# A branch of its own for each step of an expert's first layer, weight copies placed one by one, and rank operations in later experts

## The chip, the cores and the metric

The kernel runs on one core of a Trainium2 chip. The metric is the device time of one launch in microseconds (us). A core has a matrix engine (TensorE, PE in the rows, with its weight loads as PEld), three engines for elementwise work (VectorE = DVE, ScalarE = ACT, GpSimd = POOL), a queue engine (SyncE = SP), and DMA queues that move data between main memory and the on-chip buffer (SBUF). TensorE writes its products into eight banks of an accumulator memory (PSUM). Each engine works off its own list of instructions in order and waits on semaphores for the others.

## The reference

Clustered attention, then a mixture of experts over its result, then a gated layer over that. Only the middle part bears on the change:

```python
expert_idx = np.argmax(logits, axis=1)          # logits = x @ w_gate, x is 1536 x 512
...
for i in range(N):                              # first come, first served
    e = expert_idx[i]
    if counts[e] < capacity:                    # capacity 384
        disp[e, counts[e]] = x[i]; pos[i] = counts[e]; counts[e] += 1; keep[i] = True
h = np.maximum(np.einsum('ecd,edf->ecf', disp, w1), 0.0)   # w1: 8 x 512 x 1024
y = np.einsum('ecf,efd->ecd', h, w2)                       # w2: 8 x 1024 x 512
out[i] = gate_w[i] * y[expert_idx[i], pos[i]]              # for kept tokens
```

So there are eight experts of two layers each, 512 to 1024 with a Relu and 1024 to 512, and each token goes through one of them. All data are float32.

## The kernel before

The attention takes the first 270 us or so, the experts run from 284 to 476 us, and the gated layer (`g`, `v` and `o` in the rows) follows.

**Products.** To keep float32's precision each operand is held as a high part and a low part (names ending in h and l, or an index 0 and 1 in `X` and `H`), and a product is the sum of high by high, high by low and low by high. An expert with up to 208 tokens streams high and low side by side, 2 x 208 columns (or 2 x 176, if it has up to 176 tokens), so that one pass of the high weights gives two partial results, and a pass of the low weights over the high part adds to the first (`both`, lines 877 and 878). What is left of such a *merged* step is to add the two halves: ScalarE copies the second half out of PSUM (`half`, line 902) and VectorE adds it to the first (line 903). An expert with more tokens takes the *wide* form with 384 columns and three passes (`prod`, line 869). The number of tokens is only known at run time, so every engine branches on it (`arms`, lines 855 and 858). In this data experts 0, 3, 5 and 6 take the form for 208, experts 1, 2 and 4 that for 176, and expert 7 the wide one.

**An expert.** The first layer has four steps of two 128-column blocks each (`hp`). `l1` runs two steps in one branch: products and half additions of both, and only then, for both, the Relu into the high part of `H` on ScalarE (line 915) and the low part of `H` on VectorE (line 919). Between the two calls stand the transposes of the next expert's token rows (`xt`, tile `xp`, line 840, ScalarE and VectorE copies into `X` at lines 845 and 846) and the weight copies. The second layer has two steps (`yp`), each in a branch of its own (`l2`): products, half addition, and the high and low part of the result `Y` (lines 932 and 936). A second-layer product takes the eight 128-row blocks of `H` in order, and so each `yp` reads first what the first step of the first layer made, and last what its last step made.

**Weights.** An expert has eight chunks of 128 x 1024 weights: 0 to 3 make `W1`, 4 to 7 make `W2` (4 and 5 for the first `yp`, 6 and 7 for the second). `split` takes one: a ScalarE copy rounds it to the high part (line 813), a subtraction gives the low part (line 814) on VectorE for `W1` and on GpSimd for `W2`, and SyncE then loads a later chunk into the raw buffer that came free (line 804). The gathered token rows of the next expert (`xr`, 768 KB) are requested on ScalarE's queue at the start of each expert (line 825).

**Order.** There is no planner: each engine takes its instructions as the code is written. `run` writes for each expert: `l1` of steps 0 and 1, `split` 4 and 5, `l1` of steps 2 and 3, (in expert 5 the products of `tokens`), in expert 0 the rank operations, `xt` of the next expert, `split` 6 and 7, `l2` step 0, `split` 0 and 1 of the next expert, `l2` step 1, `split` 2 and 3 of the next expert. The rank operations are 8 short VectorE instructions (`ranks`, lines 712 to 718, on 128 x 96 and 128 x 12 elements) that number the tokens, and 7 more (`invert`, lines 731 to 743) that prepare the inverse list; nothing needs them before `hots` and `tokens` in expert 5.

**PSUM.** `hp`, `xp` and `yp` share one ring of four buffers, so that a step waits until the buffer of four allocations earlier has been read out.

## Time and profile before

| | |
|---|---|
| median of 3 runs | 783.03 us (782.71 to 783.65) |
| profiled execution | 781.34 us, of which 779.6 us from the first to the last instruction |
| mean granted TensorE clock | 0.996 |
| TensorE busy | 747.8 us, 96% of the span |
| VectorE, ScalarE, GpSimd busy | 513.4, 397.9, 268.7 us (66%, 51%, 34%) |
| experts, 284.0 to 476.4 us | 192.4 us, TensorE busy 180.5 |

The profiled execution is one launch. Its rows give start and length of instructions; in brackets stands how long the engine sat idle before one and what ended that. A busy TensorE row may overlap the next, so lengths of stretches on it are best taken from start to start. The profiled execution's own time is 1.7 us under the median of the runs, and 1.7 us of it lie outside the span.

### The profile page before, as it was taken

What the parts mean: (1) busy time and instruction counts of PE and PEld (TensorE: products, weight loads), DVE (VectorE), ACT (ScalarE), POOL (GpSimd) and SP (SyncE); (2) the same over time, 40 slices, a digit from 0 to 9 for tenths busy, and PEclk for the clock granted to TensorE, in tenths of its full rate; (3) what the DMA queues carried; (4) which work ended last, traced back from release to release, by engine and by line L of the source; (5) the groups of instructions that cost most, each with busy time, mean ns of one, the idle gap of its engine ahead of it and who ended that gap; (6) DMA issues with size and microseconds to landing.
All of it is one profiled execution on the core that took longest, in us unless ns stands there. A gap on an engine that the chain in (4) does not pass through costs nothing.

```text
span 779.6 us, 12354 instructions
## 1 busy us (share of the span) xinstructions
PE 747.8 (96%) x4311; PEld 622.9 (80%) x4311; DVE 513.4 (66%) x881; ACT 397.9 (51%) x744; POOL 268.7 (34%) x244
## 2 busy tenths in 40 slices
PE   7999999999999987999999999999999999999996
PEld 6777777777777677999999998788888888888885
DVE  5677878788787747556655555777676766767433
ACT  5776777786776535567666633354222222222110
POOL 6121220210220275443492452444323333233244
PEclk9999999999999999999999999999999999999999
DMA  8847857626532263687777543323112222110012
GB/s 204 209 104 210 205 178 212 158 60 165 121 124 67 82 219 121 207 258 245 235 246 230 191 137 109 104 86 106 57 55 71 66 67 69 55 54 1 1 54 108
DMA packets 93337, 102.34 MB, mean 131 GB/s; under 512 B 30304, under 2 KB 77408, under 8 KB 93248
## 3 DMA queue, kind: packets, MB, share of 16 engines
q1 hardware_dynamic: 88384, 89.33, 39.9%
q0 software_dynamic: 1920, 6.29, 2.1%
q10 hardware_dynamic: 2944, 5.54, 2.0%
q8 instruction: 55, 0.90, 0.5%
q14 instruction: 34, 0.28, 0.1%
HBM read 68.21 MB, written 12.58 MB: 104 GB/s over the span
## 4 chain that ended last, share of the span: by engine, by line
PE 47%; POOL 5%; DVE 4%; issue 3%; DMA 2%; ACT 2%; POOLq 0%; ACTq 0%; SPq 0%; DVEq 0%
PE o L1102 12%; PE v L1082 11%; PE g L1082 11%; PE hp L877 4%; POOL W2l L814 4%; PE hp L869 2%; PE yp L869 2%; PE yp L877 2%; PE hp L878 2%; DMA raw<-in_moe_w 1%; PE yp L878 1%; DVE cb L1060 1%; POOL out L1113 1%; DMA xr<-moe_rows 0%; DMA moe_rows<-x,rslot 0%
## 5 line engine op out<-in xcount | busy, mean ns | idle before, releaser
L814 POOL TENSOR_TENSOR W2l<-raw,W2h 128x1024 fp32r<-128x1024 f32 x32 | 76.5, 2415 | 86.5 <-ACT W2h L813 86.4
L342 DVE TENSOR_REDUCE nm<-s 128x1 f32<-128x768 f32 x96 | 91.1, 949 | 11.6 <-PE s L339 10.6
L352 ACT ACTIVATE P<-s,nm 128x768 f32<-128x768 f32 x96 | 86.6, 902 | 13.3 <-DVE nm L342 10.3
L368 PE MATMUL t<-ident,P 128*128 128x128 f32 x576 | 81.1, 274 | 0.8 <-ACT PT L371 0.6
L1091 POOL TENSOR_TENSOR ghl<-u,ghh 128x512 fp32r<-128x512 f32 x36 | 50.0, 1389 | 75.3 <-ACT ghh L1090 75.3
L368 PEld LDWEIGHTS t<-ident,P 128*128 128x128 f32 x576 | 68.5, 140 | 7.8 <-DVE PT L373 2.3
L877 PE MATMUL yp<-H,W2h 128*128 128x416 f32 (+1 forms) x224 | 67.7, 369 | 6.7 <-DVE X L846 3.5
L387 PE MATMUL acc<-PT,ldv 128*64 128x384 f32 x384 | 69.7, 495 | 0.0
L877 PE MATMUL hp<-X,W1h 128*128 128x416 f32 (+1 forms) x224 | 65.2, 362 | 2.0 <-issue 1.3
L339 PE MATMUL s<-Ak,Aq 128*128 128x384 f32 x192 | 58.5, 386 | 3.4 <-ACT P L352 3.1
L1110 DVE TENSOR_TENSOR acc<-o,acc 128x512 f32<-128x512 f32 x60 | 41.2, 692 | 31.0 <-PE o L1102 31.0
L371 ACT COPY PT<-t 128x384 f32<-128x384 f32 x96 | 45.8, 477 | 29.6 <-PE t L368 29.4
L1088 DVE TENSOR_TENSOR u<-sg,g 128x512 f32<-128x512 f32 x36 | 24.7, 687 | 54.1 <-ACT sg L1087 54.1
L878 PE MATMUL yp<-H,W2l 128*128 128x208 f32 (+1 forms) x224 | 57.6, 257 | 2.1 <-POOL W2l L814 1.8
L1090 ACT CAST ghh<-u 128x512 fp32r<-128x512 f32 x36 | 22.4, 622 | 67.6 <-DVE u L1089 67.6
L878 PE MATMUL hp<-X,W1l 128*128 128x208 f32 (+1 forms) x224 | 56.0, 250 | 0.0
L373 DVE COPY PT<-t 128x384 f32<-128x384 f32 x96 | 52.3, 545 | 0.9 <-PE t L368 0.9
L339 PEld LDWEIGHTS s<-Ak,Aq 128*128 128x128 f32 x192 | 29.0, 189 | 28.3 <-ACT P L352 20.2
L339 PE MATMUL s<-kB,qB 80*128 80x384 f32 (+1 forms) x192 | 50.3, 342 | 1.0 <-ACT kB L274 0.7
L877 PEld LDWEIGHTS yp<-H,W2h 128*128 128x128 f32 x224 | 42.8, 191 | 8.6 <-ACT H L915 4.3
L1060 DVE SCALAR_TENSOR_TENSOR cb<-raw,cb 128x512 uint32<-128x512 uint32 x36 | 47.4, 1318 | 1.2
L387 PEld LDWEIGHTS acc<-PT,ldv 128*64 128x64 f32 x384 | 24.9, 136 | 28.8 <-issue 27.9
(251 smaller groups left out, 1866.4 us busy)
## 6 DMA issues: line engine op xcount, KB each, us to landing
raw<-in_moe_w SPq DMA_DIRECT2D x64, 512.0 KB, 4.4
Ak<-Hk SPq DMA_DIRECT2D x32, 192.0 KB, 4.1
moe_rows<-zero SPq DMA_DIRECT2D x8, 768.0 KB, 5.4
raw<-in_moe_w_gate SPq DMA_DIRECT2D x12, 512.0 KB, 3.5
raw<-in_moe_w_val SPq DMA_DIRECT2D x12, 512.0 KB, 3.5
raw<-in_moe_w_out SPq DMA_DIRECT2D x12, 512.0 KB, 3.7
xr<-moe_rows ACTq DMA_DIRECT2D x7, 768.0 KB, 6.7
ldq<-in_q SPq DMA_DIRECT2D x16, 192.0 KB, 3.9
```

The lines of the kernel that those rows point to most:

```text
L339: nc.tensor.matmul(ps[:, c, 0:HS], lhsT=ql[:, qs], rhs=kr[:, c * HS:(c + 1) * HS], start=a == 0, stop=a == 1)
L342: nc.vector.tensor_reduce(out=nm, in_=ps[:, :, 0:HS], axis=AX.XY, op=ALU.max, negate=True)
L352: nc.scalar.activation(out=P, in_=ps[:, :, 0:HS], func=AF.Exp, bias=nm, accum_out=self.pairs[n]["sum"][:, i, r:r + 1])
L368: nc.tensor.transpose(ps[:, jj, :], P[:, a, jj * 128:(jj + 1) * 128], self.ident)
L373: nc.vector.tensor_copy(PT[:, js, cs], ps)
L387: nc.tensor.matmul(acc[c * D:(c + 1) * D], lhsT=v[:, c * HJ + j], rhs=PT[:, c * HJ + j, :], start=j == 0, stop=j == HJ - 1, tile_position= ...
L814: (nc.vector if i < 4 else nc.gpsimd).tensor_tensor(out=l, in0=t, in1=h.bitcast(F32), op=ALU.subtract)
L877: self.nc.tensor.matmul(out[:, :, 0:w], lhsT=W[0][:, k, cols], rhs=mov[:, :, k, 0:w], start=k == 0, stop=False)
L878: self.nc.tensor.matmul(out[:, 0, 0:w], lhsT=W[1][:, k, cols], rhs=mov[:, 0, k, 0:w], start=False, stop=k == ks - 1)
L1060: v.scalar_tensor_tensor(out=b, in0=Hw, scalar=0xC0000000, in1=b, op0=ALU.bitwise_and, op1=ALU.bitwise_or)
L1082: nc.tensor.matmul(p, lhsT=W[a], rhs=self.Y[b][:, k, ts], start=i == 0, stop=i == 3 * self.KD - 1)
L1102: nc.tensor.matmul(p[t], lhsT=h[a][:, fc, t * 128:(t + 1) * 128], rhs=W[b][:, fc], start=fc == 0 and i == 0, stop=fc == 1 and i == 2)
```

## The change

`l1` now takes one step. Its branch first does the Relu and low part of the step in front (`hidden(mp - 1)`), then the products and half addition of its own step. The last step's Relu and low part get a branch of their own. `split` 4 stands behind step 0, `split` 5 behind step 1, `split` 6 behind step 3, in front of the last `hidden`. `xt` makes all twelve transposes first and then copies both buffers in one branch instead of two. `split` 7 and chunk 0 of the next expert stand in front of `l2` step 0; chunks 1 and 2 between the two steps of `l2`, chunk 3 behind. `ranks` moves from expert 0 to expert 1 and `invert` to expert 2, both between chunk 2 and `l2` step 1. In the wide form Relu and low part take both column blocks in one instruction.

```diff
--- before.py
+++ after.py
@@ -832,33 +832,35 @@
 
     def xt(self, e, cnt):
         nc = self.nc
+        banks = []
         for kp in range(self.KD // 2):
             ps = self.bank("xp")
             for kk in range(2):
                 c = (kp * 2 + kk) * 128
                 for t in range(self.nt):
                     nc.tensor.transpose(ps[:, kk, t * 128:(t + 1) * 128], self.xr[e][:, t, c:c + 128], self.ident)
-            ks = slice(kp * 2, kp * 2 + 2)
-
-            def body(w):
-                h, l = [self.X[:, i, ks, 0:w] for i in range(2)]
+            banks.append(ps)
+
+        def body(w):
+            for kp, ps in enumerate(banks):
+                h, l = [self.X[:, i, 2 * kp:2 * kp + 2, 0:w] for i in range(2)]
                 nc.scalar.copy(out=h, in_=ps[:, :, 0:w])
                 nc.vector.tensor_tensor(out=l, in0=ps[:, :, 0:w], in1=h.bitcast(F32), op=ALU.subtract)
 
-            with self.tc.If(cnt > MERGED[-1]) as c:
-                body(WIDE)
-            with c.Else():
-                body(MERGED[-1])
-
-    def arms(self, cnt, wide, merged):
+        with self.tc.If(cnt > MERGED[-1]) as c:
+            body(WIDE)
+        with c.Else():
+            body(MERGED[-1])
+
+    def arms(self, cnt, body):
 
         with self.tc.If(cnt > MERGED[1]) as c:
-            wide(WIDE)
+            body(WIDE)
         with c.Else():
             with self.tc.If(cnt > MERGED[0]) as d:
-                merged(MERGED[1])
+                body(MERGED[1])
             with d.Else():
-                merged(MERGED[0])
+                body(MERGED[0])
 
     def prod(self, out, W, m, mov, w):
 
@@ -877,65 +879,60 @@
             self.nc.tensor.matmul(out[:, :, 0:w], lhsT=W[0][:, k, cols], rhs=mov[:, :, k, 0:w], start=k == 0, stop=False)
             self.nc.tensor.matmul(out[:, 0, 0:w], lhsT=W[1][:, k, cols], rhs=mov[:, 0, k, 0:w], start=False, stop=k == ks - 1)
 
-    def group(self, cnt, W, steps, mov, name, high, low):
-
-        nc = self.nc
-
-        banks = [self.bank(name) for s in steps]
-        halves = [self.p2.tile([128, 2, MERGED[-1]], F32, name="half") for s in steps]
-
-        def wide(w):
-            for s, ps in zip(steps, banks):
-                for m in range(2):
-                    self.prod(ps[:, m], W, 2 * s + m, mov, w)
-                for m in range(2):
-                    high(2 * s + m, 1, ps[:, m:m + 1, 0:w], w)
-                for m in range(2):
-                    low(2 * s + m, 1, ps[:, m:m + 1, 0:w], w)
-
-        def merged(w):
-            sums = []
-            for s, ps, t in zip(steps, banks, halves):
-                for m in range(2):
-                    self.both(ps[:, m], W, 2 * s + m, mov, w)
-                ab = ps.rearrange("p m (a t) -> p m a t", a=2)[:, :, :, 0:w]
-                nc.scalar.copy(out=t[:, :, 0:w], in_=ab[:, :, 1])
-                nc.vector.tensor_tensor(out=ab[:, :, 0], in0=ab[:, :, 0], in1=t[:, :, 0:w], op=ALU.add)
-                sums.append((2 * s, 2, ab[:, :, 0], w))
-            for a in sums:
-                high(*a)
-                low(*a)
-
-        self.arms(cnt, wide, merged)
-
-    def l1(self, steps, cnt):
-        nc = self.nc
-
-        def high(m, n, s, w):
-            nc.scalar.activation(out=self.H[:, 0, m:m + n, 0:w], in_=s, func=AF.Relu)
-
-        def low(m, n, s, w):
-            h, l = [self.H[:, i, m:m + n, 0:w] for i in range(2)]
-            nc.vector.scalar_tensor_tensor(out=l, in0=s, scalar=0.0, in1=h.bitcast(F32), op0=ALU.max, op1=ALU.subtract)
-
-        self.group(cnt, self.W1, steps, self.X, "hp", high, low)
+    def view(self, ps, w):
+        return ps[:, :, 0:w] if w == WIDE else ps.rearrange("p m (a t) -> p m a t", a=2)[:, :, 0, 0:w]
+
+    def products(self, ps, half, W, s, mov, w):
+
+        nc = self.nc
+        for m in range(2):
+            (self.prod if w == WIDE else self.both)(ps[:, m], W, 2 * s + m, mov, w)
+        if w < WIDE:
+            t = half[:, :, 0:w]
+            nc.scalar.copy(out=t, in_=ps.rearrange("p m (a t) -> p m a t", a=2)[:, :, 1, 0:w])
+            nc.vector.tensor_tensor(out=self.view(ps, w), in0=self.view(ps, w), in1=t, op=ALU.add)
+
+    def hidden(self, mp, ps, w):
+
+        nc = self.nc
+        h, l = [self.H[:, i, 2 * mp:2 * mp + 2, 0:w] for i in range(2)]
+        nc.scalar.activation(out=h, in_=self.view(ps, w), func=AF.Relu)
+        nc.vector.scalar_tensor_tensor(out=l, in0=self.view(ps, w), scalar=0.0, in1=h.bitcast(F32), op0=ALU.max,
+                                       op1=ALU.subtract)
+
+    def result(self, dp, ps, off, w):
+
+        nc = self.nc
+        to = nc.s_assert_within(off, 0, self.rt.N + 256 - w, skip_runtime_bounds_check_because="more than 256 tokens") \
+            if w > 256 else off
+        h, l = [t[:, 2 * dp:2 * dp + 2, ds(to, w)] for t in self.Y]
+        nc.scalar.copy(out=h, in_=self.view(ps, w))
+        nc.vector.tensor_tensor(out=l, in0=self.view(ps, w), in1=h.bitcast(F32), op=ALU.subtract)
+
+    def half(self):
+        return self.p2.tile([128, 2, MERGED[-1]], F32, name="half")
+
+    def l1(self, mp, cnt, last):
+
+        ps, half = self.bank("hp"), self.half()
+
+        def body(w):
+            if last is not None:
+                self.hidden(mp - 1, last, w)
+            self.products(ps, half, self.W1, mp, self.X, w)
+
+        self.arms(cnt, body)
+        return ps
 
     def l2(self, dp, cnt, off):
-        nc = self.nc
-
-        def y(m, n, w):
-            to = nc.s_assert_within(off, 0, self.rt.N + 256 - w, skip_runtime_bounds_check_because="more than 256 tokens") \
-                if w > 256 else off
-            return [t[:, m:m + n, ds(to, w)] for t in self.Y]
-
-        def high(m, n, s, w):
-            nc.scalar.copy(out=y(m, n, w)[0], in_=s)
-
-        def low(m, n, s, w):
-            h, l = y(m, n, w)
-            nc.vector.tensor_tensor(out=l, in0=s, in1=h.bitcast(F32), op=ALU.subtract)
-
-        self.group(cnt, self.W2, [dp], self.H, "yp", high, low)
+
+        ps, half = self.bank("yp"), self.half()
+
+        def body(w):
+            self.products(ps, half, self.W2, dp, self.H, w)
+            self.result(dp, ps, off, w)
+
+        self.arms(cnt, body)
 
     def run(self, hook):
         nc, rt, E = self.nc, self.rt, self.E
@@ -969,27 +966,32 @@
             then = count(1, e + 1, None, rt.CP) if e + 1 < E else None
             if e == 5:
                 rt.hots(self.p1)
-            self.l1([0, 1], cnt)
-            self.split(e, 4)
-            self.split(e, 5)
-            self.l1([2, 3], cnt)
+            ps = None
+            for mp in range(4):
+                ps = self.l1(mp, cnt, ps)
+                if mp < 2:
+                    self.split(e, 4 + mp)
+            self.split(e, 6)
             if e == 5:
                 rt.tokens(self.bank("xp")[:, 0, 0:2 * rt.B * rt.J])
-            if e == 0:
-                rt.ranks(self.p1)
-                rt.invert(self.p1)
+            self.arms(cnt, lambda w: self.hidden(3, ps, w))
             if e + 1 < E:
                 self.xt(e + 1, then)
-            self.split(e, 6)
             self.split(e, 7)
-            for dp in range(2):
-                if e + 1 == E and dp:
-                    hook(1)
-                if e + 1 == E and not dp:
-                    hook(0)
-                self.l2(dp, cnt, off)
-                self.split(e + 1, 2 * dp)
-                self.split(e + 1, 2 * dp + 1)
+            self.split(e + 1, 0)
+            if e + 1 == E:
+                hook(0)
+            self.l2(0, cnt, off)
+            self.split(e + 1, 1)
+            self.split(e + 1, 2)
+            if e + 1 == E:
+                hook(1)
+            if e == 1:
+                rt.ranks(self.p1)
+            if e == 2:
+                rt.invert(self.p1)
+            self.l2(1, cnt, off)
+            self.split(e + 1, 3)
             cnt = then
         hook(2)
 
```

On VectorE, around the rank operations of expert 0 before (`rtt`, `rrank`, `rof` are their tiles; `X` is the next expert's tokens):

```order
L919 SCALAR_TENSOR_TENSOR H<-hp,H 128x2x176 x2
L858 UNCONDITIONAL_BRANCH
L712 TENSOR_TENSOR rtt<-roh,roff_3559 128x96
...
L718 TENSOR_TENSOR rrank<-rch_3967,rrd 128x12
L731 TENSOR_SCALAR rhi<-rrank 128x12
...
L743 TENSOR_TENSOR rof<-req,rrow 128x12x12
L848 COMPARE_AND_BRANCH
L846 TENSOR_TENSOR X<-xp,X 128x768
```

and in expert 1 of the changed kernel, where `ranks` now stands (`invert` stands at the same place of expert 2):

```order
L910 TENSOR_TENSOR Yl<-yp,Yh 128x2x176
L860 UNCONDITIONAL_BRANCH
L814 TENSOR_TENSOR W1l<-raw,W1h 128x4x256 x2
L712 TENSOR_TENSOR rtt<-roh,roff_3559 128x96
...
L718 TENSOR_TENSOR rrank<-rch_4735,rrd 128x12
L857 COMPARE_AND_BRANCH
...
L893 TENSOR_TENSOR yp<-yp,half 128x2x176
L910 ISA
L910 TENSOR_TENSOR Yl<-yp,Yh 128x2x176
```

The rank operations stood behind the last `H` and ahead of the `X` of the next expert; they now stand behind two low weight chunks and ahead of the half addition of the second `yp`.

On ScalarE, the last two steps of expert 3's first layer before (`hp_5673` and `hp_5674` are steps 2 and 3; both `W2h` rows are chunks 4 and 5):

```order
L813 CAST W2h_3489<-raw_5368 128x4x256
L813 CAST W2h_3489<-raw_5372 128x4x256
...
L858 COMPARE_AND_BRANCH
L902 COPY half_5675<-hp_5673 128x416
L902 COPY half_5676<-hp_5674 128x416
L915 ACTIVATE H_3504<-hp_5673 128x2x208
L915 ACTIVATE H_3504<-hp_5674 128x2x208
L858 UNCONDITIONAL_BRANCH
```

and in the changed kernel (`hp_5643` and `hp_5713` are steps 2 and 3, `W2h` from `raw_5338` is chunk 6):

```order
L860 COMPARE_AND_BRANCH
L899 ACTIVATE H_3504<-hp_5643 128x2x208
L892 COPY half_5714<-hp_5713 128x416
L860 UNCONDITIONAL_BRANCH
...
L813 CAST W2h_3489<-raw_5338 128x4x256
L857 COMPARE_AND_BRANCH
...
L860 COMPARE_AND_BRANCH
L899 ACTIVATE H_3504<-hp_5713 128x2x208
L860 UNCONDITIONAL_BRANCH
```

The Relu of step 2 stood behind the half copy of step 3, and that of step 3 in the same branch; now step 2's Relu stands ahead of step 3's half copy, and step 3's in a branch behind chunk 6.

## Rows read from the trace of the kernel before

**Rows 1.** Which waits TensorE sat idle for, 284 to 480 us (total us, times, longest).

```profile
PE yp L877 <- DVE X L846: 3.5, 1, 3.5
PE yp L877 <- ACT H L915: 2.0, 4, 0.5
PE yp L878 <- POOL W2l L814: 1.8, 5, 0.7
...
PE hp L877 <- issue: 1.3, 1, 1.3
PE yp L877 <- DVE H L919: 1.0, 2, 0.5
...
PE xp L840 <- DVE rtoks L760: 0.6, 1, 0.6
```

**Rows 2.** Timeline of TensorE, experts 0 to 3 (start, length, engine, line, idle before).

```profile
300.25 0.43 PE L877 MATMUL yp<-H,W2h 128*128 128x416 f32 x1 [0.54 <-ACT H L915]
...
315.13 0.34 PE L877 MATMUL hp<-X,W1h 128*128 128x352 f32 x1
...
335.49 0.35 PE L877 MATMUL hp<-X,W1h 128*128 128x352 f32 x1
...
344.17 1.47 PE L840 MATMUL xp<-ident,xr 128*128 128x128 f32 x12
346.00 0.40 PE L877 MATMUL yp<-H,W2h 128*128 128x352 f32 x1 [0.36 <-ACT H L915]
...
355.73 0.39 PE L877 MATMUL hp<-X,W1h 128*128 128x416 f32 x1
...
365.35 1.47 PE L840 MATMUL xp<-ident,xr 128*128 128x128 f32 x12
367.37 0.43 PE L877 MATMUL yp<-H,W2h 128*128 128x416 f32 x1 [0.54 <-ACT H L915]
...
377.42 0.34 PE L877 MATMUL hp<-X,W1h 128*128 128x352 f32 x1
```

**Rows 3.** Windows, the stretch behind the rank operations (us; busy by engine; PEclk; DMA share; GB/s).

```profile
308.70:312.30 3.60, 3.51 (x13) 3.46 (x14) 2.62 (x4) 2.40 (x3) 0.00 (x0) 0.54 0.24 82
```

**Rows 4.** Timeline of VectorE, the rank operations of expert 0.

```profile
300.71 0.25 DVE L712 TENSOR_TENSOR rtt<-roh,roff 128x96 f32<-128x96 f32 x1
...
302.06 2.37 DVE L715 SCALAR_TENSOR_TENSOR rrd<-rrd,rpos 128x12 f32<-128x12 f32 x1
304.35 0.16 DVE L717 SCALAR_TENSOR_TENSOR rch<-rpos,rra 128x12 f32<-128x12 f32 x1
304.54 2.22 DVE L718 TENSOR_TENSOR rrank<-rch,rrd 128x12 int32<-128x12 f32 x1
...
308.06 1.08 DVE L846 TENSOR_TENSOR X<-xp,X 128x416 fp32r<-128x416 f32 x2
```

**Rows 5.** Timeline of GpSimd, second-layer weights of experts 0 and 2.

```profile
302.01 4.72 POOL L814 TENSOR_TENSOR W2l<-raw,W2h 128x1024 fp32r<-128x1024 f32 x2 [2.26 <-ACT W2h L813]
...
342.98 9.53 POOL L814 TENSOR_TENSOR W2l<-raw,W2h 128x1024 fp32r<-128x1024 f32 x4 [10.72 <-ACT W2h L813]
```

**Rows 6.** Timeline of VectorE, the last step of expert 3's first layer.

```profile
366.13 0.60 DVE L903 TENSOR_TENSOR hp<-hp,half 128x416 f32<-128x416 f32 x1 [0.73 <-ACT half L902]
366.64 0.58 DVE L919 SCALAR_TENSOR_TENSOR H<-hp,H 128x416 fp32r<-128x416 f32 x1
```

**Rows 7.** Timeline of VectorE and ScalarE's queue where expert 1 hands over to 2.

```profile
333.51 2.36 DVE L814 TENSOR_TENSOR W1l<-raw,W1h 128x1024 fp32r<-128x1024 f32 x2 [0.42 <-ACT W1h L813]
336.23 0.53 DVE L903 TENSOR_TENSOR yp<-yp,half 128x352 f32<-128x352 f32 x1 [0.35 <-ACT half L902]
...
336.96 0.38 ACTq L825 DMA_DIRECT2D xr<-moe_rows  x1
```

**Rows 8.** Page, DMA issues: KB each, median us from issue to landing.

```profile
xr<-moe_rows ACTq DMA_DIRECT2D x7, 768.0 KB, 6.7
```

**Rows 9.** Instructions of line 855, TensorE's sequencer (ns min/median/max, first and last start).

```profile
L855 PEldq COMPARE_BRANCH  x36: 65/214/3677, 286.0 to 473.3; - x36
```

## The prediction

> **What bounds the kernel now.** I read the page first: TensorE is busy in 96% of the span, so only its idle time can be won, unless work on it changes, and this change leaves every product as it is. Next I read which waits TensorE sat idle for in the experts [rows 1]. One is long: 3.5 us, once, in front of the second `yp` of expert 0, ended by VectorE's copy of `X`. Six of about half a microsecond end with a part of `H`, ScalarE's or VectorE's (2.0 and 1.0 us together), always at the start of the first `yp`. Five are for low second-layer weights from GpSimd. The view of waits shows only full stops, so I also took lengths from start to start [rows 2]. The two layers of a merged expert have the same number of products of the same shape. In expert 2 the first layer takes 344.17 - 335.49 = 8.68 us, the second 355.73 - 346.00 = 9.73, so 1.05 us of the second is lost. In expert 3 it is 9.62 (355.73 to 365.35) against 10.05 (367.37 to 377.42), 0.43 lost. Experts 1, 4 and 6 lose 1.0 each, read in the same way. In expert 0 the second layer takes 315.13 - 300.25 = 14.88 us, and 14.88 - 9.62 = 5.26 are lost there: 3.5 by the wait, and most of the rest behind it, where the granted clock was 0.54 of full speed, the lower of TensorE's two levels (1.2 GHz), over 308.7 to 312.3 [rows 3]; ahead of it the engine had stood idle for those 3.5 us.
>
> **Expert 0 without the rank operations.** VectorE runs them from 300.71 to 308.06 [rows 4], 7.35 us, and `X` of expert 1 stands behind them; the ring's next buffer, which the second `yp` needs, is free only when `X` has been copied. Two of the 15 instructions are over 2.2 us long, while a like one between them takes 0.16. During both GpSimd was at its two weight chunks (302.01 to 306.73) [rows 5], and the first fits into the rest of chunk one, the second into that of chunk two. Without these two delays `ranks` takes 1.35 us to 302.06 and three more of some 0.2, about 1.9 us; `invert` takes from 306.76 to 308.06, 1.3 us. Moved away, `X` is copied long before the second `yp`, TensorE doesn't stop and the clock has no reason to fall: 5.26 us won. The bound from below is 4.83 (14.88 - 10.05, if the weights cost there what they cost in expert 3).
>
> **The start of the first `yp`.** In expert 3 the last product of the first layer ends at 365.35, the transposes last 1.47 us, and `yp` starts at 367.37, 0.54 late [rows 2]. VectorE adds step 3's halves at 366.13 to 366.73 and only then makes the low parts of steps 2 and 3, one after the other [rows 6]; ScalarE's Relu of step 2 is behind the half copy of step 3 as well. The first product reads only step 0's part of `H`, but a wait counts what an engine has finished, and the branch's instructions come as one piece. In the changed order step 2's Relu and low part come before step 3's half copy and addition. What the first product then waits for is at the latest that addition, at 366.73, against the transposes' end at 366.82: the gap becomes about 0.05. Six gaps of 3.0 us in all [rows 1] become 0.3: 2.7 won. Products that need steps 2 and 3 come 1 to 3.5 us later in `yp` and are covered. Bounds: 0 (something else stands at that place) and 3.0.
>
> **Second-layer weights.** `split` 4 and 5 start one step, 2.2 to 2.4 us, earlier, and `split` 6 stands before the last Relu. GpSimd needs 9.53 us for four chunks [rows 5] and starts them in expert 2 at 342.98, 1.2 us before the first layer's end; from 2.2 us earlier it is ahead of TensorE at every chunk. This takes away the 1.0 us in experts 1, 2, 4 and 6 and the 0.43 in expert 3: 4.4, of which I take 4.2, since the first product after a stop is some hundredths longer anyway. Bounds: 1.8 (the full stops alone) and 4.4. In expert 5 the transposes wait 0.6 us for `tokens`' copy [rows 1]; it is now ahead of the last low part: 0.6 won.
>
> **What the rank operations cost at their new place.** Here the change adds a wait. At the hand-over from expert 1 to 2, the low chunks end on VectorE 0.35 us before the half addition of the second `yp` (336.23) [rows 7]. Behind that addition are `Yh` on ScalarE and, behind this in ScalarE's order, the request for the token rows `xr` at 336.96, 1.47 us after expert 2's first product at 335.49. It takes 6.7 us to land [rows 8], at 8.2 us, and the transposes want it at 8.68: 0.5 us of cover in expert 2, and with a first layer of 9.62 us 1.45 in expert 3. With 1.9 us of `ranks` ahead of the addition the request is at least 1.9 - 0.35 = 1.55 late, a stop of 1.05 us. It will be more. First, `yp` is no longer held up by weights, so its end comes some 0.8 us (most of the 1.05) sooner against VectorE's work. Second, chunk 0 of the next expert now stands ahead of the first `yp`'s half addition on VectorE, at a time when GpSimd is at chunk 7: four chunks in 9.53 us from 2.2 us sooner than 342.98 end at 350.3, 6.1 us after the first layer's end, and I take 6.8, as ScalarE copies chunk 7 behind `X`; the low chunk then takes until 8.0 (1.18 each [rows 7]), and the addition was due at 6.6: 1.4 us more, passed on to everything behind it. That makes the lag of expert 2's request 1.55 + 0.8 + 1.4 = 3.75 and the stop 3.2; I take 3.0. For `invert` (1.3 us) and expert 3 the same sum is 0.95 + 0.8 + 1.4 = 3.15, less 1.45: 1.7, and about 1.9 with the Relus of expert 3, which are late on ScalarE too. Experts 1 and 4, with chunk 0's delay alone (0.7 after an expert of 208 tokens, as its layer is longer), lose about 0.3 and 0.5. Together 5.7 us; without the collision of VectorE and GpSimd 1.85 + 0.3 = 2.2; from below zero, if VectorE gets through in time.
>
> That the two engines collide I take from [rows 4, 5]. By the Trainium skill (SBUF — State Buffer, section "SBUF: two separate sides") a VectorE instruction with two SBUF inputs and a GpSimd instruction that reads SBUF hold a shared port pair by an exclusive lock, and the one that comes second waits for the whole instruction of the first. The two long rank operations agree with it; no row here shows a `W1l` chunk against a `W2l` chunk.
>
> **At nothing.** The single branch of `xt`, the Relu and low part in one instruction in the wide form, and SyncE's loads, which each start with their `split`. Instructions on TensorE are the same; only branches are added.
>
> **Sum.** 5.26 + 2.7 + 4.2 + 0.6 = 12.8 us won, 5.7 lost at the hand-overs and in experts 2 and 3: 7.1 less; I take 6.9, as the wide form's last low part gets a little later. From the profiled execution's 781.34 this gives 774.4, and from the median of the runs, 1.69 higher, 776.1.
>
> **The rivals.**
> Rival 1, *the lag is covered*: GpSimd's chunk 7 is through in time, and `xr` lands faster than its median. Of the 5.7 us at most two are left: 783.03 - 12.8 = 770.2 to 772.3, and somewhat over where part of the first `yp` gaps stays. For it speaks that VectorE has idle time; against it the 0.35 us before the addition.
>
> Rival 2, *the clock falls in experts 2 and 3*: expert 0 shows 3.5 us of idle TensorE followed by the lower level at a price of about 5.26 - 3.5 = 1.7 us. A stop of 3.0 is near that. Once gives 777.8, twice 779.5, and a longer stop about 781. Against it: both stops are shorter than that one, and the transposes' products end them in part before the addition is through.
>
> Rival 3, *it doesn't do what it says*: the semaphores still make the first `yp` wait for the last low part and the chunks still come late. Then 5.26 and some 0.6 are won, and the lag is smaller, as `yp` is later: 783.03 - 5.9 + 2.2 = 779.3.
>
> Rival 4, *slower, by instruction fetch at the branches*: In each expert TensorE passes three more places of two compares each, and one compare of `xt` less. Of the 36 rows of the first compare in TensorE's sequencer the median is 0.214 us, and one took 3.68 [rows 9]; I take it for the one that left TensorE idle in expert 0 for 1.3 us, the row that ends with "issue" [rows 1]. If each expert had one such stop more, it would cost 8 x 1.3 = 10.4 and give 783.03 - 6.9 + 10.4 = 786.5; it decides from (6.9 + 1.6) / 1.3, 6 to 7 stops. Against it: the code to jump over is half as long at each branch as before, and the median is short.
> The Trainium skill (Runtime: NRT & Kernel Launch, section "Instruction fetch mechanics") says that a taken branch whose target isn't in the small window of instructions at hand waits for a fetch over DMA; the one long row is the only one that looks like it.
>
> **How the numbers follow.** My forecast (773.5 to 778) 0.52, rival 1 0.22, rival 2 (778 to 781) 0.13, rival 3 0.06, rival 4 0.07. The predicted time is 776.1. The range goes from 770.2, rival 1's best, to 780.5; outside are rival 4 and the worst of rival 2. What a measurement of this kernel can tell from no change is about 0.2%, 1.6 us. Faster by more than that: the first four cases, 0.90 after a small part of rivals 2 and 3; the same 0.04; slower 0.06, most of rival 4.
>
> **What would show it.** In the profile after: no wait for `X` in expert 0 and the clock at 1.00 there; the first `yp` starting within 0.1 us of the transposes' end; no waits for `W2l`; waits of TensorE's transposes for `xr` in experts 2 and 3 of 3 and 1.9 us, with `ranks` and `invert` in front of VectorE's addition; a `W1l` chunk of over 2 us beside GpSimd's chunk 7. Wrong would make it: waits marked "issue" at the steps' branches (rival 4), a clock of 0.5 in experts 2 and 3 (rival 2), or no `xr` waits at all (rival 1).

## The result: 10.6 us less, and where they are in the profile

| | before | changed |
|---|---|---|
| median | 783.34 us (782.71 to 784.08, 4 runs) | 772.72 us (771.48 to 773.51, 4 runs) |
| ratio | | 0.9863, 95% interval 0.9846 to 0.9880 |
| profiled execution | 781.34 us, span 779.6 | 772.64 us, span 770.9 |
| mean granted clock | 0.996 | 0.992 |

The time fell by 10.6 us; 6.9 had been forecast, with a range that holds the result. The first view of the changed kernel is the waits of TensorE in the experts (270 to 480 us; engine, line waited for, total us, times, longest):

```profile
PE xp L841 <- DMA xr<-moe_rows: 2.8, 4, 1.7
PE yp L879 <- DVE hp L893: 1.3, 2, 0.8
...
PE yp L879 <- ACT W2h L813: 0.4, 1, 0.4
PE g L1084 <- DVE Yl L910: 0.4, 1, 0.4
...
PE hp L879 <- DVE X L848: 0.2, 1, 0.2
```

Against [rows 1]: the stop of 3.5 us for `X` is gone, so are the stops for `H` and for `W2l`. What is new is the transposes' wait for token rows (1.7 of the 2.8 us belong to the rows of expert 0, for which both kernels wait), a first `yp` that waits for a half addition (in experts 2 and 3), and one in expert 6 that waits 0.4 us for a weight copy on ScalarE.

The second view is the timeline of TensorE, from which I took the length of each expert in start-to-start times: from its first `hp` product to that of the next expert (of expert 7, to the first `g`). "First layer" reaches to the first transpose (in expert 5 to the products of `tokens`, which come before the transposes), "between" from there to the first `yp` product, "second layer" from there to the end.

| us | e0 | e1 | e2 | e3 | e4 | e5 | e6 | e7 | sum |
|---|---|---|---|---|---|---|---|---|---|
| before | 28.07 | 20.37 | 20.24 | 21.68 | 20.32 | 23.11 | 22.24 | 33.30 | 189.34 |
| changed | 22.12 | 18.91 | 20.98 | 21.61 | 18.81 | 22.14 | 21.13 | 33.30 | 178.99 |
| first layer, before | 11.18 | 8.68 | 8.68 | 9.62 | 8.66 | 9.62 | 9.60 | | |
| first layer, changed | 10.91 | 8.92 | 9.83 | 9.96 | 8.70 | 9.62 | 9.61 | | |
| between, before | 2.02 | 2.01 | 1.83 | 2.01 | 1.98 | 3.69 | 2.02 | | |
| between, changed | 1.54 | 1.26 | 2.43 | 1.99 | 1.39 | 2.86 | 1.86 | | |
| second layer, before | 14.88 | 9.68 | 9.73 | 10.05 | 9.68 | 9.80 | 10.62 | | |
| second layer, changed | 9.67 | 8.73 | 8.72 | 9.66 | 8.72 | 9.67 | 9.66 | | |

The experts take 189.34 - 178.99 = 10.35 us less, which agrees with the 10.6 us between the medians. The two profiled executions differ by only 8.7, and that comes from the attention, which the change doesn't touch: expert 0 starts at 287.05 before and at 288.72 after. Two windows of each execution show why, first before and then the changed kernel (us; busy time of PE, PEld, DVE, ACT and POOL; at the end PEclk, DMA share, GB/s):

```profile
15.00:20.00 5.00, 2.86 (x15) 1.97 (x15) 3.88 (x6) 3.67 (x7) 2.07 (x12) 1.00 0.83 221
20.00:25.00 5.00, 4.85 (x36) 4.50 (x35) 3.15 (x5) 4.32 (x11) 1.21 (x2) 1.00 0.88 226
```

```profile
15.00:20.00 5.00, 3.41 (x14) 2.35 (x14) 3.82 (x6) 3.43 (x6) 2.17 (x12) 0.76 0.94 251
20.00:25.00 5.00, 5.00 (x21) 4.87 (x22) 1.89 (x4) 2.87 (x6) 0.44 (x1) 0.55 0.85 219
```

The granted clock was near TensorE's lower level (1.2 GHz) for some 6 us in one and not in the other. It goes with the execution, not with the order of the experts: of the experiments below, a version of before (9) started expert 0 at 289.21 and a version of the changed kernel (10) at 286.63. So the experiments are read by the lengths of the experts, and by ratios to before.

The third view is the hand-over from expert 1 to 2, with `ranks` at its new place. The rows are those of GpSimd, of VectorE (timeline; start, length, line, idle before), of ScalarE with its queue, and of TensorE:

```profile
321.23 4.77 POOL L814 TENSOR_TENSOR W2l<-raw,W2h 128x1024 fp32r<-128x1024 f32 x2 [0.67 <-ACT W2h L813]
```

```profile
324.24 2.84 DVE L814 TENSOR_TENSOR W1l<-raw,W1h 128x1024 fp32r<-128x1024 f32 x1 [1.18 <-ACT W1h L813]
327.00 0.52 DVE L893 TENSOR_TENSOR yp<-yp,half 128x352 f32<-128x352 f32 x1
...
332.62 0.17 DVE L715 SCALAR_TENSOR_TENSOR rrd<-rrd,rpos 128x12 f32<-128x12 f32 x1
332.71 0.16 DVE L717 SCALAR_TENSOR_TENSOR rch<-rpos,rra 128x12 f32<-128x12 f32 x1
332.91 0.17 DVE L718 TENSOR_TENSOR rrank<-rch,rrd 128x12 int32<-128x12 f32 x1
333.33 0.53 DVE L893 TENSOR_TENSOR yp<-yp,half 128x352 f32<-128x352 f32 x1 [0.25 <-issue]
```

```profile
333.89 0.46 ACT L909 CAST Yh<-yp 128x352 f32 x1 [3.44 <-DVE yp L893]
333.98 0.38 ACTq L825 DMA_DIRECT2D xr<-moe_rows  x1
```

```profile
339.57 1.63 PE L841 MATMUL xp<-ident,xr 128*128 128x128 f32 x12 [0.71 <-DMA xr<-moe_rows]
342.00 0.40 PE L879 MATMUL yp<-H,W2h 128*128 128x352 f32 x1 [0.80 <-DVE hp L893]
...
350.72 0.39 PE L879 MATMUL hp<-X,W1h 128*128 128x416 f32 x1
```

The low part of chunk 0 takes 2.84 us where one takes 1.18 [rows 7]: GpSimd was at its last two chunks from 321.23 to 326.00. The same happens at this place in all seven merged experts (2.58 to 2.84 us). `L715` and `L718`, over 2.2 us each in [rows 4], take 0.17 now that GpSimd rests. In experiments 1 and 9, where the rank operations stand beside GpSimd's chunks again, two of them are long again, but not the same two (`L712` twice, 1.64 and 2.22 us; `L714` and `L715`, 2.35 and 2.32): it is the place and not the operation. The addition of the second `yp` comes at 333.33, the request for the rows at 333.98, 4.24 us after expert 2's first product (329.74), the rows land 5.5 us later, the transposes start, and the first `yp` comes another 2.4 us later, held by an addition.

### The profile page after: what moved, and what is told of

The parts are those of the page before. It is cut to its first block, busy times and chain, and to the rows that moved or that the text cites. A ratio compares the mean times of both kernels' runs of the same rounds, so it can differ in the third digit from the quotient of the medians.

```text
span 770.9 us, 12615 instructions
## 1 busy us (share of the span) xinstructions
PE 748.9 (97%) x4311; PEld 625.8 (81%) x4311; DVE 518.1 (67%) x875; ACT 396.6 (51%) x738; POOL 267.9 (35%) x244
## 4 chain that ended last, share of the span: by engine, by line
PE 50%; DVE 4%; ACT 4%; issue 3%; DMA 2%; POOL 1%; ACTq 0%; DVEq 0%; SPq 0%; POOLq 0%
PE o L1104 12%; PE v L1084 11%; PE g L1084 11%; PE yp L879 3%; PE hp L879 3%; PE hp L871 2%; PE yp L871 2%; DMA xr<-moe_rows 2%; PE yp L880 2%; PE hp L880 1%; ACT W1h L813 1%; PE xp L841 1%; ACT W2h L813 1%; DVE cb L1062 1%; POOL out L1115 1%
## 5 line engine op out<-in xcount | busy, mean ns | idle before, releaser
L879 PE MATMUL yp<-H,W2h 128*128 128x416 f32 (+1 forms) x224 | 65.3, 363 | 1.7 <-DVE hp L893 1.3
L814 DVE TENSOR_TENSOR W1l<-raw,W1h 128x1024 fp32r<-128x1024 f32 x32 | 49.1, 1562 | 14.7 <-ACT W1h L813 14.4
L880 PE MATMUL yp<-H,W2l 128*128 128x208 f32 (+1 forms) x224 | 56.0, 250 | 0.0
L1062 DVE SCALAR_TENSOR_TENSOR cb<-raw,cb 128x512 uint32<-128x512 uint32 x36 | 45.4, 1260 | 1.2
```

The costliest lines, as they stand in the source:

```text
L814: (nc.vector if i < 4 else nc.gpsimd).tensor_tensor(out=l, in0=t, in1=h.bitcast(F32), op=ALU.subtract)
L879: self.nc.tensor.matmul(out[:, :, 0:w], lhsT=W[0][:, k, cols], rhs=mov[:, :, k, 0:w], start=k == 0, stop=False)
L880: self.nc.tensor.matmul(out[:, 0, 0:w], lhsT=W[1][:, k, cols], rhs=mov[:, 0, k, 0:w], start=False, stop=k == ks - 1)
L1062: v.scalar_tensor_tensor(out=b, in0=Hw, scalar=0xC0000000, in1=b, op0=ALU.bitwise_and, op1=ALU.bitwise_or)
```

## The experiments

Each is set against the changed kernel's experts (178.99 us), and its ratio to before against 0.9863.

**1. The rank operations back in expert 0.**

```diff
             self.arms(cnt, lambda w: self.hidden(3, ps, w))
+            if e == 0:
+                rt.ranks(self.p1)
+                rt.invert(self.p1)
...
-            if e == 1:
-                rt.ranks(self.p1)
-            if e == 2:
-                rt.invert(self.p1)
```

> The changed kernel with the rank operations back in expert 0, in front of the transposes of expert 1. Theory A (the rank operations in front of X cost expert 0 its 5 us, and at their new place they cost experts 2 and 3 about 1.9 and 0.8 us): expert 0's second layer goes from 9.67 to 14 to 15 us, with the granted clock near 0.5 behind the stop; expert 2 falls from 20.98 to about 18.9 and expert 3 from 21.61 to about 20.8; in all 2 to 3 us slower than the changed kernel. Theory B (expert 0's gain comes from the other reordering, and the delay in experts 2 and 3 from the weight chunks): expert 0 stays near 22 us, experts 2 and 3 stay at 21.0 and 21.6, the time the same.

Measured: 775.51 us, ratio 0.9902 (0.9878 to 0.9926); experts 181.17. The total is what theory A forecast, and experts 2 and 3 came down as expected, to 18.85 and 20.86. But expert 0 did not suffer: its second layer stayed at 9.66 us. Expert 1 did, with 24.82 instead of 18.91 us. Its TensorE rows:

```profile
314.45 0.35 PE L880 MATMUL hp<-X,W1l 128*128 128x176 f32 x1 [0.83 <-DVE W1l L814]
324.14 2.50 PE L841 MATMUL xp<-ident,xr 128*128 128x128 f32 x12 [2.94 <-DMA xr<-moe_rows]
```

Neither theory holds as written, and theory A's total is right by luck. The rank operations do cost 5.9 us where they stand in expert 0, but one expert later: they delay the additions, and with them the request for the rows, to 5.69 us after expert 1's first product.

**2. The kernel before with the rank operations in experts 1 and 2.**

```diff
-            if e == 0:
-                rt.ranks(self.p1)
-                rt.invert(self.p1)
...
+                if e == 1 and dp:
+                    rt.ranks(self.p1)
+                if e == 2 and dp:
+                    rt.invert(self.p1)
                 self.l2(dp, cnt, off)
```

> The kernel before with one thing changed: ranks in expert 1 and invert in expert 2, in front of the half addition of the second yp. Theory A: expert 0 gains 4.8 to 5.3 us, and since the second layer is still held up by weights there, experts 2 and 3 lose less than in the changed kernel, 0 to 1 us; the ratio to before is 0.993 to 0.995 (5.5 to 4 us). Theory B: under 1 us.

Measured: 779.30 us, ratio 0.9955 (0.9941 to 0.9969); experts 186.08, 3.26 less than before. Expert 0 gained 4.78 (28.07 to 23.29), expert 2 lost 1.55 (20.24 to 21.79), expert 3 nothing. This is theory A, with a price in expert 2 above its upper bound. The request came 3.11 us after the first product instead of 1.47, which is 1.64 later, near the 1.55 of the prediction's lower bound. The rows landed about 8.9 us after that product, some 0.2 after the transposes had been due, but TensorE was later than that already: it had waited 0.83 us for a low chunk that stands behind the rank operations on VectorE. So the price came mainly by VectorE and not by the rows.

**3. The request for token rows 10 us earlier.**

```diff
-            self.rows(e + 1)
+            if e == 0:
+                self.rows(1)
...
                 self.xt(e + 1, then)
+                self.rows(e + 2)
```

> The changed kernel with the request for token rows moved forward, from the start of each expert to right behind the transposes of the expert in front, some 10 us earlier. Theory A1, the one of the prediction (TensorE stops in experts 1 to 3 because the rows land late): the stops of 0.24, 1.15 and 0.34 us in front of the transposes go, and the kernel gains about 1.7 us. Theory A2 (behind the rows the chain half copy, addition, Relu on ScalarE and VectorE is as late): the transposes start on time but the first yp doesn't, expert 2 stays at 20.9 us and expert 3 at 21.6, the gap between them growing by what the stop loses; the gain is 0.2 to 0.5 us.

Measured: 774.87 us, ratio 0.9898 (0.9873 to 0.9923); experts 179.92. This is theory A2, and worse: expert 2 took 21.31, expert 3 22.30 us. TensorE no longer waits for rows there but for additions, twice in each; in expert 2:

```profile
340.95 0.87 PE L841 MATMUL xp<-ident,xr 128*128 128x128 f32 x6 [0.78 <-DVE hp L893]
342.62 0.40 PE L879 MATMUL yp<-H,W2h 128*128 128x352 f32 x1 [0.80 <-DVE hp L893]
```

**4. Relu and low part of step 2 behind step 3, as before.**

```diff
-            if last is not None:
+            if last is not None and mp < 3:
                 self.hidden(mp - 1, last, w)
             self.products(ps, half, self.W1, mp, self.X, w)
+            if mp == 3:
+                self.hidden(mp - 1, last, w)
```

> The changed kernel with Relu and low part of step 2 behind the products and half addition of step 3, as before. Theory A (the gap in front of the first yp is that order): the gap returns in each of the seven merged experts, where it isn't covered by something later, 0.5 to 0.75 us each, 3 to 4.5 us in all. Theory C (the gap went because the branches are smaller or the transposes come in one piece): nothing changes, within 0.5 us.

Measured: 774.35 us, ratio 0.9886 (0.9861 to 0.9911); experts 179.65. In experts 0, 1 and 6 "between" is 2.04, 1.85 and 2.03 us, the 2.02, 2.01 and 2.02 of before: there the order is the whole of the gap, or nearly so. In expert 4 (1.27) the gap is hidden behind a later landing of rows (first layer 9.24), and in expert 2 "between" even falls to 2.00 behind a first layer of 10.10. So theory A has the cause right and its sum wrong: 0.7 us in all, since where the rows or the chain are late already the order costs nothing more.

**5. The rank operations on GpSimd.** The products and sums go to GpSimd at the same places, with these two lines as the pattern (the sum over eight experts is made by halves, as additions). The conversion to integers, the split of the rank into two parts and one compare stay on VectorE, all with `invert`. The lines are cut from a longer edit:

```diff
-            v.tensor_reduce(out=r[i], in_=t, axis=AX.X, op=ALU.add)
+            g.tensor_tensor(out=t[:, :, 0:4], in0=t[:, :, 0:4], in1=t[:, :, 4:8], op=ALU.add)
...
-        v.tensor_tensor(out=self.of[:, :, 0], in0=eq, in1=tile.unsqueeze(2).to_broadcast(t3), op=ALU.mult)
+        nc.gpsimd.tensor_tensor(out=self.of[:, :, 0], in0=eq, in1=tile.unsqueeze(2).to_broadcast(t3), op=ALU.mult)
```

> [...] Theory A2 (in experts 2 and 3 VectorE's and ScalarE's chain is late by the length of the rank operations on VectorE): expert 2 falls from 20.98 to about 19.0, like experts 1 and 4 (18.91, 18.81), expert 3 from 21.61 to 21.0 to 21.3, in all 2.3 to 2.7 us faster than the changed kernel. Theory A3 (the chain is late by the weight chunks on VectorE that wait for GpSimd, the rank operations fit in): experts 2 and 3 fall by less than 0.5 us each.

Measured: 771.80 us, ratio 0.9841 (0.9824 to 0.9859), not to be told from the changed kernel's; experts 178.57. In expert 2 the addition for which the first `yp` had waited comes 10.02 us after the expert's first product (first row), against 11.59 in the changed kernel (second row), so the chain had been late by nearly the length of the rank operations:

```profile
339.70 0.52 DVE L901 TENSOR_TENSOR hp<-hp,half 128x352 f32<-128x352 f32 x1
```

```profile
341.33 0.52 DVE L893 TENSOR_TENSOR hp<-hp,half 128x352 f32<-128x352 f32 x1
```

Expert 3 fell by 0.38 to 21.23, within theory A2's range. But expert 2 took 21.73, because of this row:

```profile
341.42 0.84 PE L849 MATMUL xp<-ident,xr 128*128 128x128 f32 x6 [2.90 <-DMA xr<-moe_rows]
```

The request came at 2.30, not 4.24 us, after the first product, and landed 9.3 us later, where the changed kernel's landed after 5.5.

**6. Chunk 0 of the next expert behind the first `yp`.**

```diff
-            self.split(e + 1, 0)
...
             self.l2(0, cnt, off)
+            self.split(e + 1, 0)
             self.split(e + 1, 1)
```

> The changed kernel with the next expert's chunk 0 behind the first yp, with chunks 1 and 2, and not ahead of it. Theory A2/A3, collision part (the low part of chunk 0 is on VectorE while GpSimd works on chunk 7 and takes 2.8 us for 1.2, and this makes the half addition and all behind it late): no low chunk is over 1.3 us any more, the half addition of the first yp is 0.9 us sooner, and experts 2 and 3 gain 0.3 to 1.0 us each, experts 1 and 4 up to 0.2. Rival (chunk 0's work is only moved behind, and the chain has it there): within 0.3 us, since what is won in front of the first yp is lost between the two.

Measured: 777.45 us (772.88 to 782.87), ratio 0.9902 (0.9865 to 0.9939); the profiled execution is the longest one, with 188.38 in the experts and a granted clock of 0.93 in three of them. In the experts no low `W1` chunk takes over 1.31 us any more. In expert 1, counted from the first product of the first `yp`, that step's half addition comes at 5.14 instead of 5.99 us, as forecast, but that of the second `yp` at 12.62 instead of 12.32. The requests for rows in experts 1 to 6 came later than in the changed kernel (2.75 against 1.98 us in expert 1, 4.53 against 4.24 in expert 2), the rows landed after 6.7 to 9.4 us, and the transposes waited for rows five times, once ahead of expert 0 as in all versions. So the rival has the mechanism: what is won in front of the first `yp` is lost between the two. With that scatter the size of the loss stays open.

**7. The second-layer weights at their old places.**

```diff
-                if mp < 2:
-                    self.split(e, 4 + mp)
-            self.split(e, 6)
+                if mp == 1:
+                    self.split(e, 4)
+                    self.split(e, 5)
...
+            self.split(e, 6)
             self.split(e, 7)
```

> The changed kernel with chunks 4 and 5 both behind step 1 of the first layer and 6 with 7 behind the transposes, as before. Theory A (the second layer's waits for low weights came from these places): the second layers of experts 1, 2, 4 and 6 are 0.9 to 1.0 us longer again and that of expert 3 0.4, where the chain in front of them isn't late already; 3 to 4.4 us slower than the changed kernel. Rival (the waits went since the first yp's start moved): under 1 us.

Measured: 789.82 us, ratio 1.0082 (1.0062 to 1.0101); experts 195.54, 16.6 more than the changed kernel and 6.2 more than before. The rows are TensorE's waits for low second-layer weights, and GpSimd's last two chunks in expert 0:

```profile
PE yp L880 <- POOL W2l L814: 9.8, 7, 2.0
```

```profile
303.41 5.72 POOL L814 TENSOR_TENSOR W2l<-raw,W2h 128x1024 fp32r<-128x1024 f32 x2 [2.96 <-ACT W2h L813]
```

This is theory A in its direction, not in its size. `yp` starts sooner in the new order, and now GpSimd is held up by VectorE's chunk 0 as well, which runs from 305.26 to 306.90 (5.72 us for two chunks, against 4.72 [rows 5]). Not all of the 16.6 us are waits for weights: the rows have 9.8 of these, and the granted clock was 0.93 in two of the experts. The other edits need the earlier weights.

**8. The rank operations behind the second `yp`.**

```diff
-            if e == 1:
-                rt.ranks(self.p1)
-            if e == 2:
-                rt.invert(self.p1)
             self.l2(1, cnt, off)
+            if e == 1:
+                rt.ranks(self.p1)
+            if e == 2:
+                rt.invert(self.p1)
```

> The changed kernel with ranks and invert behind the second yp of the same experts instead of in front of its half addition. Theory A1 (late request for the token rows): the request of expert 2 comes 1.9 us sooner, that of expert 3 1.3, and expert 2 gains about 1.2 and expert 3 0.3. Theory A2 (chain on VectorE): the first half addition of the next expert stays as late as before, and experts 2 and 3 stay within 0.3 us of 20.98 and 21.61.

Measured: 772.63 us, ratio 0.9862 (0.9845 to 0.9878); experts 176.91. The requests came at 2.27 and 2.18 us instead of 4.24 and 3.43. Expert 2 fell by 0.71 to 20.27, expert 3 by 0.49 to 21.12: between the theories, nearer to A1. The rows still landed late in expert 2, at 9.5 instead of 9.7 us, as they took 7.2 us this time. The timed runs don't tell it from the changed kernel.

**9. The kernel before with both `X` copies in one branch.** The edit is that of `xt` in the change; its main lines:

```diff
-            ks = slice(kp * 2, kp * 2 + 2)
+            banks.append(ps)
...
-            def body(w):
+        def body(w):
+            for kp, ps in enumerate(banks):
```

> The kernel before with one change alone: the transposes of the next expert first, then both X copies in one branch. The rank operations stay in expert 0, in front of X. Theory R (the stop in expert 0 needs two things: the rank operations in front of X, and a second yp that takes the buffer of the first transposes; with one branch it takes that of the first layer's last step): the stop of 3.5 us in front of the second yp and the low clock behind it go, expert 0 falls from 28.07 to about 23, and expert 1 pays instead, since the half additions, Yh and the row request stand behind the rank operations too: 3 to 5 us more than 20.37, by a late landing of the rows. In all within 2 us of before. Theory S, the one of the prediction (X must be copied before the second yp): expert 0 stays at 28 us, the time is that of before.

Measured: 783.78 us, ratio 0.9989 (0.9966 to 1.0011); experts 189.99. Expert 0 fell from 28.07 to 23.91 with the rank operations where they were, and expert 1 rose from 20.37 to 24.92. VectorE and TensorE at this place:

```profile
309.94 1.08 DVE L848 TENSOR_TENSOR X<-xp,X 128x416 fp32r<-128x416 f32 x2
310.94 0.59 DVE L905 TENSOR_TENSOR yp<-yp,half 128x416 f32<-128x416 f32 x1
```

```profile
313.12 0.42 PE L879 MATMUL hp<-X,W1h 128*128 128x352 f32 x1 [1.09 <-ACT W1h L813]
314.38 0.35 PE L880 MATMUL hp<-X,W1l 128*128 128x176 f32 x1 [0.83 <-DVE W1l L814]
325.25 1.50 PE L841 MATMUL xp<-ident,xr 128*128 128x128 f32 x12 [0.52 <-DMA xr<-moe_rows]
328.52 0.40 PE L879 MATMUL yp<-H,W2h 128*128 128x352 f32 x1 [1.77 <-DVE H L921]
```

`X` is even later than it was (309.94 against 308.06 [rows 4]), yet the second `yp` runs on. This is theory R, and theory S is wrong. The buffers bear it out: in the kernel before as built, the second `yp` of expert 0 lies in the PSUM banks of its first `xp`, and here in those of the first layer's last step. The additions, the weights and the rows of expert 1 still stood behind the rank operations, so the bill went to expert 1.

**10 and 11. Both remedies together, for a faster kernel.** The diffs are those of 5 and 3, and for the last also of 8.

> The changed kernel with the rank operations on GpSimd and the request for token rows right behind the transposes, both in one. Theory A1+A2 (experts 2 and 3 are held up by two things one behind the other, the chain on VectorE and ScalarE and the landing of the rows, so that either one alone gains little): all stops in front of the transposes and the first yp go, experts 1, 2 and 4 take 18.8 to 18.9, expert 3 20.8 and expert 6 20.8, the experts in all about 175.2 instead of 179.0, the ratio to before about 0.981. Rival (the earlier request delays the weight chunks by as much): the experts stay at 178 or more.

Measured: 772.68 us (768.63 to 775.84), ratio 0.9861 (0.9837 to 0.9885); experts 177.07 in the fastest execution, so neither the 175.2 of the theory nor the rival's 178. Expert 2 took 19.32, but expert 3 22.29, where it took 21.23 in experiment 5: its chain is late again. The first delay of it that the rows show is this one of ScalarE in expert 2, a wait for a raw weight chunk:

```profile
346.72 1.05 ACT L821 CAST W1h<-raw 128x1024 fp32r<-128x1024 f32 x1 [0.89 <-DMA raw<-in_moe_w]
```

Four such waits for `W1` chunks make 1.8 us in the experts, and four make 2.4 in experiment 3; the changed kernel and experiment 5 have none for `W1`.

> As the run before, and the remaining rank operations behind the second yp. Theory A1+A2: expert 2 and 3 are at their clean length already, so nothing more is won, within 0.5 us of the run before. If expert 3 still waits for VectorE's remaining conversion and compare, up to 0.6 us less.

Measured: 773.03 us, ratio 0.9850 (0.9827 to 0.9872); experts 179.64. Nothing more was won, but not because the experts were clean: expert 3 took 22.45, TensorE waits for additions at five first `yp`, 3.7 us in all, and ScalarE waits six times for `W1` chunks, 7.6 us. None of the versions is shown to beat the changed kernel.

## Why the prediction was right, and where its steps were not

The time came out at 772.7, inside the range but a little below my own forecast (773.5 to 778), and the steps tell why. By experts, the prediction's terms are put together here against what the profile shows (us, changed less before):

| | e0 | e1 | e2 | e3 | e4 | e5 | e6 |
|---|---|---|---|---|---|---|---|
| predicted | -5.7 | -1.2 | +1.7 | +1.0 | -1.0 | -0.6 | -1.5 |
| measured | -5.95 | -1.46 | +0.74 | -0.07 | -1.51 | -0.97 | -1.11 |

**Second-layer weights: right.** Predicted 4.2; the second layers of experts 1 to 6 are 4.4 us shorter and at their clean length. Experiments 2 and 9, without the earlier places, keep the waits for `W2l`, and experiment 7 brings them back in the new order. It also shows that the other edits depend on the earlier places, which I had not seen.

**The first `yp`: right in its cause and in its size.** I took 2.7 us for six gaps, 0.45 each. Where the transposes start on time, the stretch from the first transpose to the first `yp` is 0.48 us shorter in expert 0 (2.02 to 1.54) and 0.59 in expert 4 (1.98 to 1.39). These are the rows of expert 4, with no idle time before the `yp`:

```profile
381.03 1.50 PE L841 MATMUL xp<-ident,xr 128*128 128x128 f32 x12
382.42 0.40 PE L879 MATMUL yp<-H,W2h 128*128 128x352 f32 x1
```

The 0.75 of expert 1 (2.01 to 1.26) is not all won: its transposes start 0.25 us late, as the first layer's 8.92 show. In experts 2 and 3 the late addition took the gain away, and in expert 6 most of it went to the wait for a weight copy. Experiment 4 shows the order of Relu and addition as the cause.

**Expert 0: right number, half the mechanism.** Predicted 5.26, measured 5.21 in the second layer. In the kernel before the mechanism is as I wrote: experiment 2, with the rank operations moved and nothing else, shortens that layer to 10.05, by 4.83, my bound from below. But I wrote that the next buffer is free only when `X` has been copied, as if that were fixed, and put the single branch of `xt` at nothing. The ring doesn't go strictly by four allocations, as I had it: experiment 9 shows that the edit to `xt` alone changes the buffer and takes the stop out of expert 0, and experiments 1 and 9 that the rank operations then cost expert 1 4.5 to 5.9 us. Moving them away is what makes the gain stay: it is worth 181.17 - 178.99 = 2.2 us in the experts, net of what they cost in experts 2 and 3.

**The hand-overs: the term that was mis-sized.** I took 3.0 and 1.9 us for experts 2 and 3. Put in the same way (what remains over the clean length) expert 2 lost 20.98 - 18.85 = 2.1 and expert 3 21.61 - 20.86 = 0.75, with the clean length from experiment 1. Experts 1 and 4, which I took at 0.3 and 0.5, lost next to nothing (18.91 and 18.81 against the 18.79 of expert 1 in experiment 8). So about 3.0 us were lost where I had taken 5.7, which is most of what the forecast was short by. Three steps of the sum were too long: GpSimd's chunk 7 ended 6.2 us after the first transpose, not 6.8, and the low chunk 7.3, not 8.0; the request in expert 2 came at 4.24 us, where 1.47 + 3.75 = 5.22 had been the sum; and the rows landed after 5.5, not 6.7. How fast the rows land was luck, as the last paragraph of this section shows. That the collision happens is as predicted, with 2.84 us. By the lock that the Trainium skill states (SBUF — State Buffer, section "SBUF: two separate sides") the chunk would wait for the whole of GpSimd's instruction; the trace agrees, as the chunk, begun at 324.24, ends 1.08 us after GpSimd does, close to the 1.18 that it takes alone.

My sum for the stop also took the landing of the rows for the one thing behind the late addition. Experiments 3, 5 and 8 show two limits, one close behind the other: the landing, and the chain of half copy, addition and Relu. If one is taken away, the other is there.

**The rivals.** Rival 1 (the lag is covered, 770.2 to 772.3) comes nearest to the time, but not to what happened: the lag is there, at about half the size I gave it. Rival 2 fell: the granted clock was 1.00 in all of experts 2 and 3 (329.7 to 372.3 us), where the stops were under 1 us. Had the stops been the 3.0 us of my sum, it would have been open: in experiment 1 a stop of 2.94 us was followed by a granted clock of 0.58, in experiment 5 one of 2.90 by 1.00. These are the windows, first of the changed kernel's experts 2 and 3, then of the stretch behind the stop in experiment 1 and in experiment 5:

```profile
329.70:350.70 21.00, 19.49 (x142) 18.71 (x141) 14.87 (x27) 13.45 (x23) 9.64 (x6) 1.00 0.80 245
350.70:372.30 21.60, 20.93 (x142) 20.38 (x141) 15.89 (x27) 14.05 (x23) 9.52 (x4) 1.00 0.77 249
```

```profile
324.00:327.00 3.00, 2.86 (x15) 2.89 (x16) 1.35 (x3) 1.67 (x4) 2.67 (x2) 0.58 0.83 279
```

```profile
341.30:344.00 2.70, 2.58 (x21) 2.61 (x22) 1.01 (x3) 2.45 (x5) 1.33 (x1) 1.00 0.61 197
```

Rivals 3 and 4 fell: the stops went, and none of the changed kernel's waits in the experts is marked as "issue". One such stop still comes in experiment 3 (1.19 us, in expert 0), as one did before: one in an execution, not one in each expert.

**What stays open.** How long the rows take to land is not explained: in expert 2 it was 5.5 us in the changed kernel, 9.3 and 7.2 in experiments 5 and 8, and 6.7 before. Which other transfers were under way was not varied alone. Why one stop of 2.9 us was followed by the lower clock and the other wasn't is open too.

## What to carry to other kernels

A stop that names one instruction may be the place where a whole engine's delay is first felt. If that stop is taken away by another buffer or branch, the delay is paid one stage later, so move the work and not only the wait. Work for an engine with small reserves is best priced by what stands behind it in order on that engine and on the next, and by a second limit just behind the first: if moving one brings nothing, look for the other before calling the first harmless. Edits to an order are not a sum: with the earlier weights the second layers became 4.4 us shorter than before, but taking these out of the new order alone cost 16.6 us.

## What the runs showed of the hardware that was not expected

A transfer of 768 KB, requested in the same way, landed after 4.5 to 9.4 us over these kernels, and in the three versions that requested it 10 us sooner ScalarE waited four to six times for `W1` chunks, 1.8 to 7.6 us in all; of the others only experiment 7 has such waits. VectorE and GpSimd hold each other up in both directions: a low chunk on VectorE took 2.84 instead of 1.18 us, two on GpSimd 5.72 instead of 4.72 us. Two stops of TensorE of equal length, 2.94 and 2.90 us, were followed by the lower and by the higher clock. And the lower clock came early in the attention, at 18 to 25 us, in some executions of either order and not in others (0.50 against 1.00 over 18 to 24 us), at a price of about 2 us.
